# Giving the denominator-spreading matmul 128 rows, 124 of them zero, instead of four, in a linear-attention and MoE kernel

## The chip, the cores and the metric

The kernel runs on one core of a Trainium2 chip. The metric is the device time of one execution in microseconds (us); lower is better.

## The reference

Linear attention over 8 batches of 8 heads (576 tokens, head size 64), followed by a gated feed-forward layer with a three-tap convolution over tokens.

```python
def phi(x):                                   # 64 -> 128, then exp of plus and minus
    proj = np.einsum('bhsd,df->bhsf', x, w_phi)
    proj = proj - np.max(np.abs(proj), axis=-1, keepdims=True)
    return np.concatenate([np.exp(proj), np.exp(-proj)], axis=-1)
q_p, k_p = (phi(q), phi(k))
kv = np.einsum('bhsf,bhsd->bhfd', k_p, v)
z = np.sum(k_p, axis=2)
num = np.einsum('bhsf,bhfd->bhsd', q_p, kv)
den = np.einsum('bhsf,bhf->bhs', q_p, z)[..., None] + 1e-06
x = num / den                                 # heads side by side: [8, 576, 512]
h = np.maximum(x @ w_in, 0.0)                 # 512 -> 1024
conv_out = sum(conv_w[k] * shifted(h, k) for k in range(3))
out = (h * sigmoid(conv_out)) @ w_out         # 1024 -> 512
```

## The kernel before

Names in the profile are those of the program's tiles. Attention works in quads of four heads (two pairs), 16 quads in all, each in five groups of tokens. For each group the tensor engine projects keys and queries (`kp`, `qp`), the vector engine takes the greatest magnitude off, the scalar engine takes exponentials (`ke`, `qe`), queries are transposed (`tp`), keys are multiplied with values (`kv`), and queries with the result (`nm`). Row 64 of `nm` holds the denominators. To keep accuracy, most operands are split into a rounded part and the rest (`..h` and `..l`, type fp32r), and a product takes three matmuls.

For each of the 32 pairs of heads `x_process` then divides. The denominators have been gathered by DMA into `den`; the vector engine takes the reciprocal `rc` and splits it in two parts, and four small DMAs lay these out as four rows of 576 tokens in `rr`: high part of head 0, high part of head 1, low part of head 0, low part of head 1. A matmul with the stationary matrix `sel_r` (four rows of ones and zeros, 128 columns) then adds high and low parts and spreads each head's reciprocal over the 64 partitions that hold the head's numerators. It does so twice per pair, for two chunks of 290 tokens, into the PSUM tile `rb`: 64 such matmuls in the kernel. The vector engine multiplies `num` by `rb` into `xf`, and `xf` is split into `xh` and `xl`, the moving operands of the MoE.

The MoE takes 16 chunks of 288 tokens. `h_part` makes 8 tiles `hp`, each by 12 matmuls of 128 rows, 128 columns and 290 tokens; `conv_process` makes the convolution and the gate on the vector, scalar and GpSimd engines; `o_part` makes 4 tiles `op`, each by 24 matmuls of 288 tokens.

The weights `w_in` and `w_out` arrive as float64. In the first part of the run they are loaded in 16 pieces (`w_r`) and rounded to float32 by the vector, scalar and GpSimd engines (`w_t`), next to the first batch's attention.

The order on each engine is decided ahead: the parts are generators, and a loop merges them, with attention a set number of instructions ahead of the MoE. A scheduler then places each instruction by its own estimates of time, so that a change in one instruction can move others. All loads go out on SyncE's queue (SP), in order. The tile `selr_f`, which receives the four rows of `sel_r` from memory, shares its two buffers (tag `qr`) with the raw queries from the second batch on.

Of the kernel before, what the change touches and what calls it, by code (L numbers as in the profile page):

```python
# [7 lines left out]
F32 = mybir.dt.float32  # L8
# [10 lines left out]
P = 128  # L19
NQ = 2            # quads (four heads each) per batch  # L20
TC = 288          # tokens per MoE chunk
HW = TC + 2       # tokens of h computed per MoE chunk (one token of halo, even width)
VW = D + 1
NH = 11           # tiles of h
# the order of work
WINDOW = 13       # chains of attention in flight
LAT = 1.7         # latencies stretched by
TAIL_US = 24      # of the MoE's products, what is left when attention's are done
AHEAD = 300       # instructions by which attention goes before the MoE that it was merged with
# quads whose products are in float32, as long as the tensor engine has time, so that nothing has to be split  # L30
NQ_F32 = 2        # q's projections
NKV_F32 = 2       # the products with kv


@with_exitstack
def kernel(
    ctx: ExitStack,
    tc: tile.TileContext,
    qT: bass.AP,     # [B, NQ, 128 = (i, d), 2*S], the last 64 tokens of either pair in the middle
    kT: bass.AP,     # likewise  # L40
    vt: bass.AP,     # [B, NQ, 128, 20*65]
    wbd: bass.AP,    # [128, 256] block diagonal of w_phi
    w_in: bass.AP,   # [8 = (4 c, 2 halves), 128, 512], in float64 twice as many words
    conv_w: bass.AP,  # [128, (8, 3)], likewise
    w_out: bass.AP,  # [8, 128, DM], likewise
    ident: bass.AP,  # [128, 128]
    selr: bass.AP,   # [4, 128]
    out: bass.AP,    # [B, 4, 128, S]
):
# [7 lines left out]
    def split(src, hi, lo, eng_hi, eng_lo):  # L57
        """hi: src rounded to 12 significant bits, lo: the exact rest."""
        if eng_hi is nc.scalar:
            nc.scalar.activation(out=hi, in_=src, func=AF.Copy)  # L60
        elif eng_hi is nc.gpsimd:
            nc.gpsimd.tensor_scalar(out=hi, in0=src, scalar1=1.0, scalar2=0.0, op0=ALU.mult, op1=ALU.add)  # L62
        else:
            nc.vector.tensor_copy(out=hi, in_=src)
        eng_lo.tensor_tensor(out=lo, in0=src, in1=hi.bitcast(F32), op=ALU.subtract)  # L65

# [1 line left out]
    def load_const(ap, shape, name):  # L68
# [10 lines left out]
    idn = load_const(ident, [P, P], "idn")  # L79
    selr_f = sb.tile([4, P], F32, name="selr_f", tag="qr", bufs=2)  # L80
    nc.sync.dma_start(out=selr_f, in_=selr)
    sel_r = cp.tile([4, P], F32R, name="sel_r")
    nc.vector.tensor_copy(out=sel_r, in_=selr_f)

    # Weights that come as float64 arrive as raw 64-bit words, of a high half (sign, 11 bits
    # of exponent, 20 of fraction) and a low half (32 of fraction). The engines build
    #   power = +-2^e   and   w = (1.fraction) * power, rounded to float32 once.
    # Exponents below float32's give zero, those above it infinity or NaN.
    bias_e = cp.tile([P, 1], F32, name="bias_e")
# [17 lines left out]
    def weight_split(src, n, hi, lo):  # L107
        """src: [128, 512] weights in DRAM (float32, or the words of float64)."""
        name = f"w{n}_"
        if src.dtype == F32:  # L110
            raw = sb.tile([P, 512], F32, name=f"{name}r", tag="gh", bufs=2)
            nc.sync.dma_start(out=raw, in_=src)
            split(raw, hi, lo, nc.gpsimd, nc.gpsimd)
            return
        raw = sb.tile([P, 1024], I32, name=f"{name}r", tag="gh", bufs=2)
        nc.sync.dma_start(out=raw, in_=src)
        tmp = sb.tile([P, 2, 512], F32, name=f"{name}t", tag="gl", bufs=2)
        w = tmp[:, 0, :]
        float64_round(raw, w, tmp[:, 1, :])
        split(w, hi, lo, nc.scalar, nc.gpsimd)  # L120
# [22 lines left out]

# [1 line left out]
    # The parts below are processes: generators that trace some instructions and then  # L145
    # yield how long the tensor engine is held by them (pe), how long it is until the
    # next part has its operands (wait), or a condition that has to hold (until). The
    # loop at the end merges them into one order in which products of one process
    # cover the latencies of the others.
    now = [0.0]  # L150
# [13 lines left out]

# [1 line left out]
    # A quad is two pairs of heads. Its tokens come in groups: group 0 is the last 64  # L166
    # tokens of both pairs, groups 1 to 4 are 256 tokens of a pair. A tile of 128 tokens
    # holds a pair of heads, one above the other, against block diagonal weights.
    def group_columns(g):
# [15 lines left out]
    def project(n, hi, lo, b, qd, g, kind):  # L185
        """The projection of n tiles of two heads less its greatest magnitude per token and head."""
        if b == 0 and kind == "k":
            # the MoE doesn't use its banks yet
            ps = pm.tile([P, n * 256], F32, name=f"{kind}p{b}_{qd}_{g}", tag="m")
        else:  # L190
            ps = pg.tile([P, n * 256], F32, name=f"{kind}p{b}_{qd}_{g}", tag="g", bufs=4)
# [17 lines left out]
    def after(ins, trace):  # L209
        """Trace an instruction that its engine issues behind ins."""  # L210
        if ins is None:
            return trace()
        with tc.issue_after(ins.ins):
            return trace()
# [5 lines left out]
    def k_process(b, qd, g):  # L220
# [43 lines left out]
        else:  # L264
            # five groups later in the order than the queries with whose products these alternate:
            # the loads of either's weights hide behind the other's products
            kvgen[j] = products()
            set_ready(("ke", j))
            yield until(("kvd", j))
        if g == 4:  # L270
            # these take the place of the same quad's of the batch before
            u = 2 * b + qd
# [27 lines left out]
    def q_process(b, qd, g):  # L300
# [14 lines left out]
        set_ready(("tp", *divmod(j, 5)))  # L315
        # in the order (head, tile) the tokens of a head lie side by side
        tp = pg.tile([P, 2, n, P], F32, name=f"tp{b}_{qd}_{g}", tag="g", bufs=4)
# [14 lines left out]
        yield until(back("num", 1), ("kvq", b, qd), ("ke", j + 5) if paired else None)  # L332
        # pairs of heads in this group, each with its tokens' place in the tile and in the sequence
        parts = [(0, 0, 512, 64), (1, 64, 512, 64)] if g == 0 else [((g - 1) // 2, 0, (g - 1) % 2 * 256, 256)]
# [32 lines left out]
        for pr_, o, s0, w in parts:  # L367
# [3 lines left out]
            dn, nt = den[b, qd, pr_], numt[b, qd, pr_]  # L371
            # denominators in the order (16 tokens, head)
            dro = dr[D : D + 1, 2 * o : 2 * (o + w)]
# [10 lines left out]
    def x_process(b, p):  # L384
# [5 lines left out]
        with tc.high_priority():  # L390
            rc = sb.tile([72, 16], F32, name=f"rc{b}_{p}", tag="rc", bufs=2)
            nc.vector.tensor_scalar(out=dn, in0=dn, scalar1=1e-6, scalar2=None, op0=ALU.add)
            nc.vector.reciprocal(out=rc, in_=dn)
            rr = sb.tile([4, S], F32R, name=f"rr{b}_{p}", tag="rr", bufs=1)
            rhl = [sb.tile([72, 16], F32R, name=f"rc{j}{b}_{p}", tag=f"rc{j}", bufs=2) for j in range(2)]
# [19 lines left out]

# [1 line left out]
    ht = {}  # L417
# [26 lines left out]
    def conv_process(n):  # L444
        c = n % 2
        o = 0 if c == 0 else HW - TC
        for f in range(8):
# [5 lines left out]
            cv = c4[:, f, :]  # L453
            # the tap beyond the batch's first and last token falls on nothing
            nc.gpsimd.tensor_scalar(out=cv, in0=hs[:, o : o + TC], scalar1=cw[:, f, 1:2], scalar2=0.0,  # L455
# [58 lines left out]

# [1 line left out]
    chains = [(0, 0, g, "k") for g in range(5)]  # L516
    for u in range(NQ * B):
        for g in range(5):
            chains.append((*divmod(u, NQ), g, "q"))
            if u + 1 < NQ * B:  # L520
                chains.append((*divmod(u + 1, NQ), g, "k"))
    active = []    # [time, process, is a chain, lead in priority], attention's chains and what they spawn
    lead = [None]
# [12 lines left out]
    def step(p, kind):  # L536
        """Run process p up to its next pause; False when it ended."""
        for what, arg in p[1]:
# [22 lines left out]
    while moe is not None or chains or active:  # L561
        while chains and sum(1 for p in active if p[2]) < WINDOW:
            b, x, g, kind = chains.pop(0)
            # the first batch's attention goes before all else
            lead[0] = AHEAD if b > 0 else None
# [21 lines left out]
        else:  # L587
            # nothing is ready: on to the next time at which something is
            now[0] = min([t for t, _ in ta] + ([tm] if tm is not None else []))
# [56 lines left out]
```

## Time and profile before

| what | value |
|---|---|
| median of 3 runs | 849.68 us (848.51 to 853.46) |
| span of the profiled execution, first to last instruction | 848.8 us |
| what lies around the span | not shown by the profile; the median is 0.9 us above the span |
| tensor engine, matmuls (PE) | 817.7 us busy, 6414 matmuls |
| tensor engine, weight loads (PEld) | 788.2 us |
| vector engine (DVE) | 623.3 us, 1327 instructions |
| scalar engine (ACT) | 571.9 us, 1228 instructions |
| GpSimd (POOL) | 304.0 us, 466 instructions |
| mean granted clock of the tensor engine | 0.981 |

Matmuls overlap each other in the records: one of 290 tokens is shown as lasting some 0.30 us while the next begins 0.13 us after it. What one costs is therefore read from the spacing of starts, not from durations. A weight load has a row of its own (PEld), and a matmul's shape is written as rows*columns of the stationary matrix, then the moving operand.

### The profile page before, as it was taken

How to read it: one execution, taken by the hardware profiler on the slowest of the kernel's cores; microseconds unless marked ns; L12 is line 12 of the kernel's file. 1: busy time of each engine (PE TensorE's matmuls, PEld its weight loads, DVE VectorE, ACT ScalarE, POOL GpSimd, SP SyncE). 2: the span in 40 equal slices, each digit the busy share in tenths (PEclk: the TensorE clock that was granted, in tenths of full speed). 3: DMA queues.
4: the chain of work that ended last, by engine and by line, in shares of the span. 5: the costliest groups of instructions: out<-in, count | busy, mean ns of one | idle time of the engine just before them, and what ended most of it. 6: DMA issues, size and time to landing. Idle time of an engine off the chain costs nothing.

```text
span 848.8 us, 18003 instructions
## 1 busy us (share of the span) xinstructions
PE 817.7 (96%) x6414; PEld 788.2 (93%) x6414; DVE 623.3 (73%) x1327; ACT 571.9 (67%) x1228; POOL 304.0 (36%) x466
## 2 busy tenths in 40 slices
PE   7888879999999999999999999999999999999998
PEld 6867778989999999999999999999999999999998
DVE  5679999898877767776777776777687776756561
ACT  4677787787768667676777867577575876644332
POOL 4557668542442423423142332324144121211110
PEclk9799889999999999999999999999999999999999
DMA  6354331111212212112111211121121100000001
GB/s 194 112 153 125 103 118 51 49 43 53 65 41 65 60 31 68 40 55 56 49 54 47 61 35 57 46 59 54 31 68 36 48 15 22 10 29 29 22 15 49
DMA packets 56336, 49.19 MB, mean 58 GB/s; under 512 B 15028, under 2 KB 54200, under 8 KB 56248
## 3 DMA queue, kind: packets, MB, share of 16 engines
q1 hardware_dynamic: 56248, 48.05, 19.6%
q8 instruction: 51, 0.84, 0.4%
q14 instruction: 37, 0.30, 0.1%
HBM read 38.14 MB, written 9.44 MB: 56 GB/s over the span
## 4 chain that ended last, share of the span: by engine, by line
PE 80%; DVE 9%; ACT 4%; DMA 3%; issue 2%; POOL 0%; SPq 0%; DVEq 0%; POOLq 0%; ACTq 0%
PE op L491 24%; PE hp L432 22%; PE nm L356 8%; PE kv L255 8%; PE tp L320 3%; PE rb L407 2%; PE nm L348 2%; PE qp L199 2%; PE qp L200 2%; PE kp L199 2%; PE qp L201 2%; PE kp L200 2%; PE kp L201 1%; PE kv L251 1%; DMA den<-dr 1%
## 5 line engine op out<-in xcount | busy, mean ns | idle before, releaser
L460 DVE SCALAR_TENSOR_TENSOR c<-h,cw,c 128x288 f32<-128x288 f32 (+1 forms) x256 | 138.6, 550 | 38.4 <-POOL c L455 36.6
L255 PE MATMUL kv<-v,ke 128*128 128x65 f32 x1024 | 161.6, 256 | 0.0
L255 PEld LDWEIGHTS kv<-v,ke 128*128 128x128 f32 x1024 | 156.6, 196 | 4.3 <-issue 1.2
L432 PE MATMUL hp<-xh,win_hi 128*128 128x290 f32 x512 | 153.2, 301 | 1.1 <-ACT os L496 0.6
L432 PE MATMUL hp<-xl,win_hi 128*128 128x290 f32 x512 | 153.5, 300 | 0.0
L455 POOL TENSOR_SCALAR c<-h,cw 128x288 f32<-128x288 f32 x128 | 78.2, 612 | 209.3 <-ACT h L439 172.4
L432 PE MATMUL hp<-xh,win_lo 128*128 128x290 f32 x512 | 153.2, 299 | 0.0
L491 PE MATMUL op<-gh,wout_hi 128*128 128x288 f32 x512 | 152.8, 299 | 0.0
L491 PE MATMUL op<-gh,wout_lo 128*128 128x288 f32 x512 | 151.8, 297 | 0.0
L491 PE MATMUL op<-gl,wout_hi 128*128 128x288 f32 x512 | 151.8, 296 | 0.0
L62 POOL TENSOR_SCALAR kxh<-kr 128x256 fp32r<-128x256 f32 (+1 forms) x80 | 38.0, 475 | 225.7 <-PE kp L200 201.3
L65 DVE TENSOR_TENSOR ql<-qe,qh 128x512 fp32r<-128x512 f32 x112 | 80.1, 728 | 28.2 <-ACT qh L60 28.2
L432 PEld LDWEIGHTS hp<-xh,win_hi 128*128 128x128 f32 x512 | 96.7, 189 | 2.9 <-ACT os L496 1.4
L432 PEld LDWEIGHTS hp<-xh,win_lo 128*128 128x128 f32 x512 | 97.1, 190 | 1.6
L432 PEld LDWEIGHTS hp<-xl,win_hi 128*128 128x128 f32 x512 | 97.0, 189 | 1.0
L491 PEld LDWEIGHTS op<-gh,wout_hi 128*128 128x128 f32 x512 | 96.1, 188 | 0.9
L491 PEld LDWEIGHTS op<-gh,wout_lo 128*128 128x128 f32 x512 | 96.4, 188 | 0.1
L491 PEld LDWEIGHTS op<-gl,wout_hi 128*128 128x128 f32 x512 | 96.2, 188 | 0.2 <-issue 0.2
L439 ACT ACTIVATE h<-hp 128x290 f32<-128x290 f32 x128 | 52.4, 412 | 58.9 <-PE hp L432 56.3
L326 ACT ACTIVATE qe<-tp 128x512 f32<-128x512 f32 x112 | 62.0, 598 | 26.9 <-PE tp L320 22.1
L374 ACT ACTIVATE dr<-nm 1x512 f32<-1x512 f32 (+1 forms) x96 | 46.3, 482 | 48.2 <-PE nm L356 28.2
L204 DVE TENSOR_REDUCE km<-kp 128x4 f32<-128x512 f32 (+1 forms) x80 | 50.4, 631 | 33.8 <-PE kp L201 33.8
(86 smaller groups left out, 2039.1 us busy)
## 6 DMA issues: line engine op xcount, KB each, us to landing
v<-in_vt_dram SPq DMA_DIRECT2D x80, 130.0 KB
out_dram<-os SPq DMA_DIRECT2D x64, 144.0 KB
kr<-in_kT_dram SPq DMA_DIRECT2D x64, 128.0 KB
qr<-in_qT_dram SPq DMA_DIRECT2D x64, 128.0 KB
w_r<-in_w_in_dram SPq DMA_DIRECT2D x8, 512.0 KB
w_r<-in_w_out_dram SPq DMA_DIRECT2D x8, 512.0 KB
rr<-rc SPq DMA_DIRECT2D x128, 2.2 KB
kr<-in_kT_dram SPq DMA_DIRECT2D x16, 64.0 KB
```

The source lines that it names most:

```text
L62: nc.gpsimd.tensor_scalar(out=hi, in0=src, scalar1=1.0, scalar2=0.0, op0=ALU.mult, op1=ALU.add)
L65: eng_lo.tensor_tensor(out=lo, in0=src, in1=hi.bitcast(F32), op=ALU.subtract)
L204: nc.vector.tensor_reduce(out=m, in_=ps3, axis=AX, op=ALU.max, apply_absolute_value=True)
L255: ins = nc.tensor.matmul(out=kp[i][:, s, p0 : p0 + VW], lhsT=lhsT, rhs=v[:, (2 * t + i) * VW : (2 * t + i + 1) * VW], start=False, stop=(g ...
L326: nc.scalar.activation(out=e, in_=tp.rearrange("p i t s -> p i (t s)"), func=AF.Exp, scale=1.0 - 2.0 * s)
L356: ins = after(ins, lambda: nc.tensor.matmul(out=ps[:, i, o : o + w], lhsT=w_, rhs=x_, start=(k == 0), stop=(k == 5)))
L374: nc.scalar.activation(out=dro.rearrange("o (r i c) -> o i r c", i=2, c=16), in_=ps[D : D + 1, :, o : o + w].rearrange("o i (r c) -> o i r ...
L432: nc.tensor.matmul(out=ps, lhsT=w_, rhs=x_, start=(k == 0), stop=(k == 11))
L439: nc.scalar.activation(out=hs, in_=ps, func=AF.Relu)
L455: nc.gpsimd.tensor_scalar(out=cv, in0=hs[:, o : o + TC], scalar1=cw[:, f, 1:2], scalar2=0.0, op0=ALU.mult, op1=ALU.add)
L460: nc.vector.scalar_tensor_tensor(out=cv[:, lo:hi], in0=hs[:, o + j - 1 + lo : o + j - 1 + hi], scalar=cw[:, f, j : j + 1], in1=cv[:, lo:hi ...
L491: nc.tensor.matmul(out=ps, lhsT=w_, rhs=x_, start=(k == 0), stop=(k == 23))
```

## The change

`sel_r` and `rr` get all 128 partitions. Rows 4 to 127 are set to zero once, at the start; the four rows that matter are written as before. `rr` is now a single tile for the whole run, where it was allocated anew for each pair from a pool of one buffer. The conversion of `sel_r` moves from the vector engine to GpSimd, which also does the two memsets. The matmul's code is the same; its operands have 128 rows.

```diff
-    selr_f = sb.tile([4, P], F32, name="selr_f", tag="qr", bufs=2)
-    nc.sync.dma_start(out=selr_f, in_=selr)
-    sel_r = cp.tile([4, P], F32R, name="sel_r")
-    nc.vector.tensor_copy(out=sel_r, in_=selr_f)
+    selr_f = sb.tile([P, P], F32, name="selr_f", tag="qr", bufs=2)
+    nc.gpsimd.memset(selr_f, 0.0)
+    nc.sync.dma_start(out=selr_f[:4, :], in_=selr)
+    sel_r = cp.tile([P, P], F32R, name="sel_r")
+    nc.gpsimd.tensor_copy(out=sel_r, in_=selr_f)
+    rr = cp.tile([P, S], F32R, name="rr")
+    nc.gpsimd.memset(rr.bitcast(F32), 0.0)
...
-            rr = sb.tile([4, S], F32R, name=f"rr{b}_{p}", tag="rr", bufs=1)
```

The rest of the diff takes comments out. Line numbers grow by three or four: the matmul is line 407 before and 410 after.

The order of the engines changes in the first third of the program and is nearly the same from there on. At the start of SyncE's queue stood, before (`kr` and `qr` are raw keys and queries, named by batch, quad and group):

```order
L75 DMA wbd_f_70<-in_wbd_dram 128x256
L179 DMA kr0_0_0_131<-in_kT_dram 128x128
L176 DMA qr0_0_0_147<-in_qT_dram 128x128
L179 DMA kr0_0_1_139<-in_kT_dram 128x256
L176 DMA qr0_0_1_149<-in_qT_dram 128x256
L230 DMA v0_0_0_137<-in_vt_dram 128x260
L179 DMA kr0_0_2_188<-in_kT_dram 128x256
```

And now:

```order
L75 DMA wbd_f_70<-in_wbd_dram 128x256
L183 DMA qr1_0_0_853<-in_qT_dram 128x128
L180 DMA qr0_0_0_150<-in_qT_dram 128x128
L183 DMA kr0_0_0_134<-in_kT_dram 128x128
L180 DMA qr0_0_1_152<-in_qT_dram 128x256
L183 DMA kr0_0_1_142<-in_kT_dram 128x256
L234 DMA v0_0_0_140<-in_vt_dram 128x260
```

The first keys have moved from second to fourth place, behind a load of the second batch's queries. On GpSimd, a little later, among the splits of the first keys, the conversion of `sel_r` now stands:

```order
L62 TENSOR_SCALAR kxh0_0_4_306<-kr0_0_4_304 128x256
L85 CAST sel_r_81<-selr_f_78 128x128
L65 TENSOR_TENSOR kxl0_0_4_307<-kr0_0_4_304,kxh0_0_4_306 128x256
```

It delays the split behind it by its own time. On the vector engine the conversion of the weights has moved ahead of attention's work. Before, from the engine's 23rd row on (`w0_t`, `w1_t` are weights; `km`, `qs`, `ks` attention's):

```order
L206 TENSOR_TENSOR qs0_0_2_322<-qp0_0_2_317,qm0_0_2_320 128x512
L103 SCALAR_TENSOR_TENSOR cw_84<-cw_84,cw_raw_85 128x24
L96 TENSOR_SCALAR w1_t_153<-w1_r_151 128x512
L204 TENSOR_REDUCE km0_0_4_380<-kp0_0_4_373 128x4
L206 TENSOR_TENSOR qs0_0_3_329<-qp0_0_3_324,qm0_0_3_327 128x512
L204 TENSOR_REDUCE km0_1_0_391<-kp0_1_0_387 128x2
L98 TENSOR_SCALAR w0_t_121<-w0_r_119 128x512
```

And now:

```order
L210 TENSOR_TENSOR qs0_0_2_325<-qp0_0_2_320,qm0_0_2_323 128x512
L102 TENSOR_SCALAR w0_t_124<-w0_r_122 128x512
L104 SCALAR_TENSOR_TENSOR w0_t_124<-w0_r_122,w0_t_124 128x512
L100 TENSOR_SCALAR w1_t_156<-w1_r_154 128x512
L210 TENSOR_TENSOR qs0_0_3_332<-qp0_0_3_327,qm0_0_3_330 128x512
L107 SCALAR_TENSOR_TENSOR w0_t_124<-w0_t_124,w0_r_122 128x512
L208 TENSOR_REDUCE km0_0_4_383<-kp0_0_4_376 128x4
```

The lead grows: the last weight's last instruction is the vector engine's 213th before and its 177th now, 36 places earlier. From about the 1,900th of 5,662 tensor engine instructions on, the order there is the same but for single places at `rb`.

## The prediction

> **What bounds the kernel.** I read the page's busy times first, then the busy time in two stretches, split where the vector engine stops being full.
>
> ```profile
> PE 817.7 (96%) x6414; PEld 788.2 (93%) x6414; DVE 623.3 (73%) x1327; ACT 571.9 (67%) x1228; POOL 304.0 (36%) x466
> ```
>
> ```profile
> 0.00:143.50 143.50, 121.74 (x836) 110.30 (x837) 119.16 (x217) 103.35 (x222) 91.14 (x112) 0.89 0.42 125
> 143.50:849.00 705.50, 695.99 (x5580) 677.92 (x5579) 504.16 (x1111) 468.50 (x1006) 212.90 (x355) 1.00 0.16 44
> ```
>
> The columns are PE, PEld, DVE, ACT and POOL busy with their counts, then granted clock and DMA. From 143.5 us on PE is busy for 696.0 of 705.5 us at full clock, and the next engine, DVE, for 504.2 (71%). There the tensor engine is the bound, and what it saves in spacing the run saves. Before 143.5 us no engine is full all the time: the stretch is paced by loads, weight conversion and chains between engines.
>
> The affected matmul, by the view of its tile, and its count in the two stretches:
>
> ```profile
> L407 PEld LDWEIGHTS rb<-rr,sel_r x64: 181/181/185, 68.1 to 745.3; 4*128 4x128 f32 x64
> L407 PE MATMUL rb<-rr,sel_r x64: 288/396/400, 68.1 to 745.4; 4*128 4x290 f32 x64
> ```
>
> ```profile
> 143.50:849.00 705.50, 21.10 (x56) 9.88 (x56) 1.00 0.16 44
> ```
>
> So 56 of the 64 stand in the stretch that PE bounds. Their load of 181 ns is nothing special. What they cost shows only in the spacing around one. The timeline of PE, and of its weight loads, in the middle of a run of `hp` (columns: start, busy, engine, line):
>
> ```profile
> 248.03 0.29 PE L432 MATMUL hp<-xh,win_hi 128*128 128x290 f32 x1
> 248.16 0.29 PE L432 MATMUL hp<-xl,win_hi 128*128 128x290 f32 x1
> 248.38 0.40 PE L407 MATMUL rb<-rr,sel_r 4*128 4x290 f32 x1
> 248.71 0.40 PE L432 MATMUL hp<-xh,win_lo 128*128 128x290 f32 x1
> 248.94 0.30 PE L432 MATMUL hp<-xh,win_hi 128*128 128x290 f32 x1
> 249.08 0.30 PE L432 MATMUL hp<-xl,win_hi 128*128 128x290 f32 x1
> ```
>
> ```profile
> 248.03 0.19 PEld L432 LDWEIGHTS hp<-xl,win_hi 128*128 128x128 f32 x1
> 248.38 0.18 PEld L407 LDWEIGHTS rb<-rr,sel_r 4*128 4x128 f32 x1 [0.16 <-ACT ke L237]
> 248.71 0.19 PEld L432 LDWEIGHTS hp<-xh,win_lo 128*128 128x128 f32 x1
> 248.81 0.19 PEld L432 LDWEIGHTS hp<-xh,win_hi 128*128 128x128 f32 x1
> ```
>
> Ordinary `hp` start 0.13 us apart, because each one's load runs a step ahead of its matmul: the load for the matmul at 248.16 began at 248.03. `rb`'s load begins only at 248.38, with its own matmul, and the next `hp`'s load only at 248.71, again with its own matmul. The reader is to see that the lead of the loads is lost twice, going into the four-row matmul and coming out, and must be built up again. From 248.16 to 248.94 three steps take 0.78 us where three ordinary ones take 0.40: an excess of 0.38 us.
>
> **The change part by part.**
>
> *The 64 matmuls.* Moving shape and columns stay (290, 128); the rows become 128. The changed one is then of the very shape of `hp`, 128*128 with 128x290 of the same type, and the trace shows that at 0.13 us. I take an excess of zero. The lower bound is the same, since nothing here is cheaper than `hp` for that shape. The upper bound is today's excess, if the loss is not due to the rows.
>
> The excess depends on the neighbours, so I weigh three kinds. The 56 are 46 single ones and five pairs of two in a row, counted along the timeline from the first at 143.9 to the last at 745.4 us. Of the single ones, 38 stand as above, with the full 0.38, and 8 have a short neighbour after `nm` or `kv`, as here:
>
> ```profile
> 184.38 0.31 PE L356 MATMUL nm<-qh,kvl 128*65 128x256 f32 x1
> 184.62 0.40 PE L407 MATMUL rb<-rr,sel_r 4*128 4x290 f32 x1
> 184.94 0.33 PE L356 MATMUL nm<-qh,kvh 128*65 128x256 f32 x1
> 185.12 0.33 PE L255 MATMUL kv<-v,ke 128*128 128x65 f32 x2
> ```
>
> ```profile
> 375.25 0.31 PE L356 MATMUL nm<-qh,kvl 128*65 128x256 f32 x1
> 375.40 0.30 PE L432 MATMUL hp<-xh,win_hi 128*128 128x290 f32 x1
> ```
>
> 184.38 to 185.12 is 0.74 us. The same without loss: 0.15 from `nm` to an `hp` (second fence), 0.13 for the `hp` shape, 0.12 from `nm` to `kv`, the shortest such step: 0.40. Excess 0.34. A pair, and the one pair with a wait inside:
>
> ```profile
> 641.94 0.30 PE L432 MATMUL hp<-xh,win_lo 128*128 128x290 f32 x1
> 642.16 0.54 PE L407 MATMUL rb<-rr,sel_r 4*128 4x290 f32 x2
> 642.63 0.33 PE L356 MATMUL nm<-qh,kvh 128*65 128x256 f32 x1
> 642.80 0.28 PE L199 MATMUL kp<-wbd_hi,kxh 128*128 128x256 f32 x1
> ...
> 543.12 0.37 PE L407 MATMUL rb<-rr,sel_r 4*128 4x290 f32 x1 [0.47 <-DVE ks L206]
> ```
>
> 641.94 to 642.80 is 0.86 us for four steps, against 3 x 0.13 + 0.15 = 0.55: excess 0.31 for the pair. The 0.47 us in the pair at 543 is a wait for DVE and stays. Sum: 38 x 0.38 + 8 x 0.34 + 5 x 0.31 = 14.4 + 2.7 + 1.6 = 18.7 us off the stretch from 143.5 us.
>
> The Trainium skill's page "TensorEngine Tiling (Array Packing)", Key Properties, says that a change of tiling mode drains the tensor engine, which would make an excess of this kind at each side of a four-row matmul; the two late loads agree with it. Its page "TensorE: Matmul & The Clock Gate", Part 2, step 1, speaks against this change: a weight load takes as long with few rows as with 128, and its summary table has one short-row matmul at the time of a full one. The loads here, 181 ns against 0.19 us, agree with that, the spacing does not; by that rule alone neither the 18.7 nor the gain on the early ones would come, and the sum would be 851.0.
>
> *The eight early ones.* They lie at 68 to 123 us, where DVE paces; between 0 and 8 x 0.38 = 3.0 us can come from them. I take 1.0, nearer the covered end, as DVE decides there.
>
> *The first loads.* The start of the chain of waits and SP's first issues:
>
> ```profile
> 1.18 2.61 DMA kr<-in_kT_dram
> ```
>
> ```profile
> 1.18 0.42 SPq L179 DMA_DIRECT2D kr<-in_kT_dram  x1
> 1.65 0.43 SPq L176 DMA_DIRECT2D qr<-in_qT_dram  x1
> 2.12 0.43 SPq L179 DMA_DIRECT2D kr<-in_kT_dram  x1
> ```
>
> The first keys now go out two places later, at 2.12: +0.94 us on the chain.
>
> *The new GpSimd work.* Nearest rows, the old conversion of four rows and a first split of 128x128:
>
> ```profile
> L83 DVE CAST sel_r<-selr_f x1: 514/514/514, 11.8 to 11.8; 4x128 fp32r<-4x128 f32 x1
> ...
> 3.88 0.30 POOL L62 TENSOR_SCALAR kxh<-kr 128x128 fp32r<-128x128 f32 x1 [3.05 <-DMA kr<-in_kT_dram]
> ```
>
> The conversion sits in front of a split on the chain: 0.30 to 0.51 us; I take +0.4. The memset of 128x576 (4.5 times the columns of the 0.30 us row: at most 1.4 us) hides in GpSimd's 3.05 us of idle time before the first keys; without that cover it would cost the 1.4. SP's load of `selr_f` waits for the small memset, which is long over when SP reaches it.
>
> *The single `rr` tile.* The old pool had one buffer, so its four DMAs already waited for both matmuls of the pair before. Nothing is added; if it were, `rb` would wait for the landing instead.
>
> *The moved order.* Up to the point where the orders agree again each engine does the same work. Weights come earlier on DVE, attention later. I take 0, and bounds: a gain up to the 5.3 us that DVE stood before a weight in the first 60 us, a loss up to 36 displaced places at DVE's mean of 119.16 / 217 = 0.55 us, 19.8 us.
>
> ```profile
> DVE w_t L96 <- POOL win_lo L65: 5.3, 2, 3.6
> ```
>
> *Sum.* 848.8 - 18.7 - 1.0 + 0.94 + 0.4 = 830.4 us of span. The median of the runs stands 0.9 us above the profiled span; with that, 831.3 us.
>
> **The rivals.**
>
> *The loss is not due to the rows.* The load row of `rb` carries a wait of 0.16 us, and each `rb` stands behind several semaphores. If the lateness came from these, a matmul of four rows would cost what one of 128 does, and only the startup's terms would be left: 848.8 + 0.94 + 0.4 + 0.9 = 851.0. Against it: the second late load, the `hp` at 248.71, follows a matmul for which it has nothing to wait, and the step into `rb` is 0.22 to 0.24 us in all three timelines above, whatever stands before. If only the entry step (0.09 of 0.38) is a wait, 56 x 0.09 = 5.0 us stay: 836.3. The rule of the Trainium skill's page "TensorE: Matmul & The Clock Gate" on few rows stands on the side of this rival.
>
> *The startup gives it back* (the other side). The weights' lead pushes the first batches' attention back on DVE, PE starves, and the full stretch begins later. At the bound of 19.8 us the time is 831.3 + 19.8 = 851.1, slower than before. It decides from 18.4 us on. For it speaks that DVE is in order and that the tensor engine's clock was already only 0.89 there; against it, that DVE idled 143.5 - 119.2 = 24.3 us in this stretch, time which earlier weights can fill.
>
> *PE's saved time turns into waits.* If another engine held back half of it, 831.3 + 9.4 = 840.7. DVE at 71% and ACT at 66% from 143.5 us on speak against it.
>
> **How the numbers follow.** Forecast, with startup between -5 and +5 us: 0.75. Entry step stays a wait or saved time half lost: 0.11. Startup loses 5 to 14 us: 0.06. Nothing gained by the rows: 0.04. Startup at its bound: 0.02. Startup gains more than 5 us: 0.02. Likeliest 831.3; the range goes down by 5.3 and some more to 825, and up to the half-lost case, 841. A measurement of this kernel tells about 0.5%, 4.2 us, from no change. Faster takes the first, most of the second and third and the last: 0.93; same 0.05; slower 0.02.
>
> **What would show it.** `rb` should stand as 128*128 at 0.13 us spacing, its load ahead of its matmul, the next `hp` too; durations near 300 instead of 396 ns. The stretch from the first full PE to the end should be some 19 us shorter, with the same order. Its beginning should lie within 5 us of 143.5. The prediction is wrong if `rb`'s load still starts with its matmul, if PE's idle time after 143.5 us grows, or if the full stretch begins late.

## The result and the profile after

The changed kernel takes 837.6 us (median of 5), against 849.7 us before: a ratio of 0.985 (95% interval 0.982 to 0.987), some 12.5 us faster. The prediction said 831.3 us, with a range of 825 to 841.

One of the five executions, the one that was profiled, ran at a mean granted clock of 0.75 and took 957.1 us, so the ratio is that of the other four, and the profile shown here is a second one of the same kernel at the usual clock: 835.2 us of span in an execution of 837.0 us. Its busy times, from the page, and its two stretches, cut where about as many matmuls are left as at the cut before (5583 and 5580):

```profile
PE 801.9 (96%) x6414; PEld 784.3 (94%) x6414; DVE 623.7 (75%) x1326; ACT 573.1 (69%) x1228; POOL 307.5 (37%) x469
```

```profile
0.00:145.80 145.80, 121.63 (x833) 109.07 (x834) 120.63 (x221) 106.32 (x225) 95.64 (x117) 0.91 0.41 123
145.80:835.20 689.40, 680.25 (x5583) 675.19 (x5581) 503.06 (x1106) 466.82 (x1004) 211.90 (x353) 1.00 0.16 45
```

The affected matmul, by its tile:

```profile
L410 PEld LDWEIGHTS rb<-rr,sel_r x64: 186/188/288, 69.8 to 731.9; 128*128 128x128 f32 x64
L410 PE MATMUL rb<-rr,sel_r x64: 291/298/610, 69.8 to 732.0; 128*128 128x290 f32 x64
```

Three things are to be seen. The matmul's median fell from 396 to 298 ns, that of an `hp`. PE's busy time fell by 15.8 us (817.7 to 801.9), the span by only 13.6. And the stretch in which PE is full got 15.9 us shorter (705.3 to 689.4 us, to the last instruction) but began 2.3 us later.

### The profile page after: what moved, and what is told of

It reads as the page before. It is cut to its first block, busy times and chain, and to the rows that moved or that the text cites. A ratio compares the mean times of both kernels' runs of the same rounds, so it can differ in the third digit from the quotient of the medians.

```text
span 955.3 us, 18005 instructions
## 1 busy us (share of the span) xinstructions
PE 937.9 (98%) x6414; PEld 920.7 (96%) x6414; DVE 622.2 (65%) x1326; ACT 576.6 (60%) x1228; POOL 294.1 (31%) x469
## 4 chain that ended last, share of the span: by engine, by line
PE 93%; DVE 3%; ACT 2%; issue 1%; DMA 1%; POOL 0%; SPq 0%; ACTq 0%
PE op L494 26%; PE hp L435 25%; PE kv L259 10%; PE nm L360 9%; PE tp L324 4%; PE nm L352 3%; PE kp L203 2%; PE kp L204 2%; PE kp L205 2%; PE qp L204 2%; PE qp L203 2%; PE qp L205 2%; PE kv L255 2%; PE rb L410 1%; PE qp L200 1%
## 5 line engine op out<-in xcount | busy, mean ns | idle before, releaser
L259 PEld LDWEIGHTS kv<-v,ke 128*128 128x128 f32 x1024 | 181.8, 221 | 5.2
L259 PE MATMUL kv<-v,ke 128*128 128x65 f32 x1024 | 181.8, 280 | 0.0
L463 DVE SCALAR_TENSOR_TENSOR c<-h,cw,c 128x287 f32<-128x287 f32 (+1 forms) x256 | 138.6, 550 | 59.1 <-POOL c L458 57.3
L435 PE MATMUL hp<-xl,win_hi 128*128 128x290 f32 x512 | 171.0, 334 | 0.0
L435 PE MATMUL hp<-xh,win_hi 128*128 128x290 f32 x512 | 170.9, 335 | 0.1
L494 PE MATMUL op<-gh,wout_hi 128*128 128x288 f32 x512 | 170.5, 333 | 0.0
L494 PE MATMUL op<-gh,wout_lo 128*128 128x288 f32 x512 | 170.3, 333 | 0.0
L494 PE MATMUL op<-gl,wout_hi 128*128 128x288 f32 x512 | 170.3, 333 | 0.0
L435 PE MATMUL hp<-xh,win_lo 128*128 128x290 f32 x512 | 170.1, 332 | 0.0
L435 PEld LDWEIGHTS hp<-xh,win_hi 128*128 128x128 f32 x512 | 104.4, 205 | 1.0 <-ACT os L499 0.6
```

The costliest lines, as they stand in the source:

```text
L259: ins = nc.tensor.matmul(out=kp[i][:, s, p0 : p0 + VW], lhsT=lhsT, rhs=v[:, (2 * t + i) * VW : (2 * t + i + 1) * VW], start=False, stop=(g ...
L435: nc.tensor.matmul(out=ps, lhsT=w_, rhs=x_, start=(k == 0), stop=(k == 11))
L463: nc.vector.scalar_tensor_tensor(out=cv[:, lo:hi], in0=hs[:, o + j - 1 + lo : o + j - 1 + hi], scalar=cw[:, f, j : j + 1], in1=cv[:, lo:hi ...
L494: nc.tensor.matmul(out=ps, lhsT=w_, rhs=x_, start=(k == 0), stop=(k == 23))
```

## The experiments

Two theories stood at the start. A: the rows are worth the predicted 18 to 19 us, and the new order of the first third gives 5 to 7 back. B: the order is neutral, and the rows are worth only 12 to 13.

**The changed kernel again.**

> The changed kernel once more, for a profile at full clock. Both theories: 837 us, 12 to 13 below the kernel before, rb at 0.13 us spacing with its load ahead of it. Theory A (the rows are worth 18 to 19 us from 143.5 us on, as predicted, and the new order of the first third gives 5 to 7 back): the stretch that the tensor engine fills begins 5 to 7 us later than before. Theory B (the order is neutral and the rows are worth only 12 to 13): it begins at 143 to 145 us, and idle time of the tensor engine behind it grows.

It took 837.1 us, a ratio of 0.9851 (0.9835 to 0.9867) to the kernel before. The late beginning is there, but it is 2.3 us, not the 5 to 7 that A needs.

**128 rows in the old order.** With `sel_r` converted as before, the scheduler's order is that of the kernel before on every engine, but for two memsets on GpSimd.

```diff
 selr_f = sb.tile([4, P], F32, name="selr_f", tag="qr", bufs=2)
 nc.sync.dma_start(out=selr_f, in_=selr)
-sel_r = cp.tile([4, P], F32R, name="sel_r")
-nc.vector.tensor_copy(out=sel_r, in_=selr_f)
+sel_r = cp.tile([P, P], F32R, name="sel_r")
+nc.gpsimd.memset(sel_r.bitcast(F32), 0.0)
+nc.vector.tensor_copy(out=sel_r[:4, :], in_=selr_f)
+rr = cp.tile([P, S], F32R, name="rr")
+nc.gpsimd.memset(rr.bitcast(F32), 0.0)
...
-            rr = sb.tile([4, S], F32R, name=f"rr{b}_{p}", tag="rr", bufs=1)
```

> 128 rows as in the changed kernel, but the four rows of sel_r are loaded and converted as before, on the vector engine, so that every engine keeps the order of the kernel before (GpSimd has two memsets more). Theory A: 849.7 - 18.7 - 0 to 1 = 830 to 831 us, some 6 us faster than the changed kernel. Theory B: 837 us, as the changed kernel.

It took 835.1 us, ratio 0.9823 (0.9805 to 0.9841): between the two theories. The rows alone are worth 15.0 us (850.1 to 835.1, medians of the same chip).

**Four rows in the new order.** The counterpart: the changed kernel, with a matmul of four rows.

```diff
-nc.tensor.matmul(out=rb, lhsT=sel_r, rhs=rr[:, t0 : t0 + HW], start=True, stop=True)
+nc.tensor.matmul(out=rb, lhsT=sel_r[:4, :], rhs=rr[:4, t0 : t0 + HW], start=True, stop=True)
```

> The changed kernel with its order and memsets, but the matmul reads only the first four rows of sel_r and rr. Theory A: 849.7 + 5 to 7 = 855 to 857 us, slower than the kernel before. Theory B: 850 us, as the kernel before.

It took 852.2 us, ratio 1.0025 (1.0013 to 1.0037): the order alone costs 2.1 us. The four kernels make a square, and it closes:

| median, us | old order | new order | order costs |
|---|---|---|---|
| four rows | 850.1 | 852.2 | 2.1 |
| 128 rows | 835.1 | 837.1 | 2.0 |
| the rows gain | 15.0 | 15.1 | |

Both theories had a part wrong. The order costs less than A said but is not free, and the rows give more than B said but less than the 19.7 us predicted (18.7 from the full stretch and 1.0 before it).

**Where the missing gain went.** The old-order pair has the same matmuls in the same order, so the two timelines can be laid on each other one matmul at a time. Around a single `rb` in 128 rows, PE and its loads:

```profile
244.91 0.29 PE L434 MATMUL hp<-xl,win_hi 128*128 128x290 f32 x1
245.04 0.30 PE L409 MATMUL rb<-rr,sel_r 128*128 128x290 f32 x1
245.18 0.30 PE L434 MATMUL hp<-xh,win_lo 128*128 128x290 f32 x1
245.31 0.30 PE L434 MATMUL hp<-xh,win_hi 128*128 128x290 f32 x1
```

```profile
244.91 0.19 PEld L409 LDWEIGHTS rb<-rr,sel_r 128*128 128x128 f32 x1
245.04 0.19 PEld L434 LDWEIGHTS hp<-xh,win_lo 128*128 128x128 f32 x1
```

These are the matmuls that stood at 248.16 to 248.94 before. The steps are now 0.13, 0.14 and 0.13 us, and each load starts a step ahead of its matmul. The whole 0.38 us is gone here, as at most of the single places.

The sum over the full stretch is read from a matmul just ahead of its first `rb` to one just behind its last. Before:

```profile
143.55 0.33 PE L255 MATMUL kv<-v,ke 128*128 128x65 f32 x2
...
745.90 0.29 PE L491 MATMUL op<-gh,wout_lo 128*128 128x288 f32 x1
```

With 128 rows in the old order, the same two:

```profile
142.15 0.33 PE L258 MATMUL kv<-v,ke 128*128 128x65 f32 x2
...
729.94 0.29 PE L493 MATMUL op<-gh,wout_lo 128*128 128x288 f32 x1
```

602.35 us became 587.79: 14.6 us for the 56, where 18.7 were predicted. The missing 4.1 us sit at few places. The largest, in the kernel before and then with 128 rows:

```profile
162.04 0.40 PE L407 MATMUL rb<-rr,sel_r 4*128 4x290 f32 x1
...
163.01 0.29 PE L432 MATMUL hp<-xh,win_lo 128*128 128x290 f32 x1
163.23 0.40 PE L407 MATMUL rb<-rr,sel_r 4*128 4x290 f32 x1
```

```profile
160.82 0.29 PE L434 MATMUL hp<-xh,win_lo 128*128 128x290 f32 x1
162.20 0.38 PE L409 MATMUL rb<-rr,sel_r 128*128 128x290 f32 x1 [1.08 <-DVE ks L209]
```

The second `rb` now arrives 1.08 us before the vector engine has released it. The subtraction that releases it, before and then with 128 rows:

```profile
161.79 0.68 DVE L206 TENSOR_TENSOR ks<-kp,km 128x512 f32<-128x512 f32 x1
```

```profile
161.38 0.68 DVE L209 TENSOR_TENSOR ks<-kp,km 128x512 f32<-128x512 f32 x1
```

It came only 0.41 us earlier, while the tensor engine came to the second `rb` more than 2 us earlier: the `hp` ahead of it starts at 160.82 and not at 163.01 us. Of this, 1.40 us had been won before the full stretch (it begins at 142.15 and not at 143.55). So around 162 us the vector engine decides, and what the tensor engine saves there is not saved by the run. Here the two `rb` with their neighbours lose 0.69 us instead of winning 0.7. At four of the five pairs the saving is partly a wait as well. The pair that took 0.86 us for four steps at 641.94:

```profile
629.26 0.30 PE L434 MATMUL hp<-xh,win_lo 128*128 128x290 f32 x1
629.40 0.43 PE L409 MATMUL rb<-rr,sel_r 128*128 128x290 f32 x2
629.67 0.28 PE L359 MATMUL nm<-qh,kvh 128*65 128x256 f32 x1
629.94 0.36 PE L202 MATMUL kp<-wbd_hi,kxh 128*128 128x256 f32 x1
```

Up to `nm` all is as predicted (0.41 us from the `hp`). Then `kp` starts 0.27 us after `nm`, where 0.12 us would be a plain step: its sequencer stands for 0.40 us in a wait for a semaphore, from 629.49 to 629.88. The same wait was there before, from 642.16 to 642.55, and had ended by the time at which `nm` began at 642.63. The shortfalls, from the matmul-by-matmul comparison:

| place | predicted us | found us | short by |
|---|---|---|---|
| the two `rb` at 162 and 163 us | -0.72 | +0.69 | 1.4 |
| `rb` at 250.1, the next `nm` waits | -0.38 | +0.04 | 0.4 |
| three `rb` behind a `kp`, which still wait | -1.14 | -0.42 | 0.7 |
| five pairs | -1.55 | -0.96 | 0.6 |
| five `rb` between `kv` and `nm` | -1.70 | -1.39 | 0.3 |
| matmuls that are no neighbours of `rb` | 0 | +0.8 | 0.8 |

They add up to 4.2 us; the other 35 `rb` gave what was predicted, 13.3 us. In the first two rows and at four of the pairs a wait took the saving. Behind `kp` the load engine still stands idle for 0.21 us ahead of `rb`'s load with 128 rows, as it did before; the profile puts this down to the scalar engine's `qe`. Between `kv` and `nm` the price was off by a little. The last row is made of small shifts and was not followed up.

**64, 32 and 65 rows.** What is it about four rows? Three kernels with the changed kernel's order, differing from it only in the rows that the matmul reads, as in the diff above.

> The changed kernel, its matmul reading the first 64 rows. If any part of the array less than the whole loses the lead of the loads: rb's load starts with its matmul, the excess is 0.38 us as with four rows, and the time is that of new_order_4 (855 under theory A, 850 under B). If only a quarter of the rows does: the time of the changed kernel, 837 us.

> The changed kernel, its matmul reading the first 32 rows. Both: steps of 0.22 and 0.33 us as with 4 and 64 rows, 851 to 854 us. If instead a full group of rows kept the lead: 837 us.

> The changed kernel, its matmul reading the first 65 rows. If the lead of the loads is lost whenever fewer than 128 rows are used: rb at 0.22 and 0.33 us steps, 852 to 854 us as with 64 rows. If it hangs on whether the rows need the whole array (more than half): steps of 0.13 us and the changed kernel's 837 us.

The first two took 853.7 and 851.8 us, beside 852.2 with four rows; 65 rows took 833.8 us (one run each; 32 and 65 rows ran on another chip, on which the kernel before took 849.5 us instead of 850.1). The steps tell it apart from the scatter. PE and its loads with 64 rows:

```profile
277.45 0.29 PE L494 MATMUL op<-gh,wout_lo 128*128 128x288 f32 x1
277.67 0.40 PE L410 MATMUL rb<-rr,sel_r 64*128 64x290 f32 x1
278.00 0.40 PE L494 MATMUL op<-gh,wout_hi 128*128 128x288 f32 x1
278.24 0.30 PE L494 MATMUL op<-gl,wout_hi 128*128 128x288 f32 x1
```

```profile
277.67 0.18 PEld L410 LDWEIGHTS rb<-rr,sel_r 64*128 64x128 f32 x1 [0.17 <-issue]
278.00 0.19 PEld L494 LDWEIGHTS op<-gh,wout_hi 128*128 128x128 f32 x1
```

The same place with 65 rows:

```profile
270.11 0.29 PE L494 MATMUL op<-gh,wout_lo 128*128 128x288 f32 x1
270.24 0.29 PE L410 MATMUL rb<-rr,sel_r 65*128 65x290 f32 x1
270.37 0.30 PE L494 MATMUL op<-gh,wout_hi 128*128 128x288 f32 x1
270.51 0.29 PE L494 MATMUL op<-gl,wout_hi 128*128 128x288 f32 x1
```

```profile
270.11 0.19 PEld L410 LDWEIGHTS rb<-rr,sel_r 65*128 65x128 f32 x1
270.24 0.19 PEld L494 LDWEIGHTS op<-gh,wout_hi 128*128 128x128 f32 x1
```

64 rows cost 0.79 us for three steps, 65 rows 0.40. With 32 rows the steps are those of 64, 0.22, 0.33 and 0.24 us. The border lies between 64 and 65 rows: with 65 the matmul stands in the stream like any other. The Trainium skill's page "TensorEngine Tiling (Array Packing)" lists arrays of 32 and 64 rows as modes beside the whole, and its Key Properties say that a change of mode drains the engine; loads that wait for the matmul ahead of them, on both sides, at 4, 32 and 64 rows and not at 65 or 128, agree with it. No record names a mode, so that this is what happens inside the engine is argued and not shown. What the pairs add is that the price hangs on the change from one kind of matmul to the other: in the pair at 642 us the first four-row load starts late, with its matmul, but the second starts at 642.27, 0.13 us ahead of its matmul at 642.40, as after any late load, and the load of `nm` behind them is late again. And the pair at 745 us, between `op`, gave back 0.38 us for its two matmuls, as a single place does.

**Which part of the order costs the 2 us.** The profiles of the square can be compared by the number of matmuls done. Up to the 839th all four have run as many into each tile. It starts at 143.69 and 147.45 us with four rows, in the old and the new order, and at 142.29 and 146.26 with 128: the new order is 3.8 and 4.0 us behind. At the 2,462nd, an `rb` in all four, it is 1.9 and 2.4 us behind, and 2.1 and 2.4 at the last. So the startup loses some 4 us, and about half of them come back soon after. Time at half clock does not explain it alone: in the first 160 us it is 30.7 and 27.3 us with four rows, 23.9 and 27.3 with 128.

To find the part of the order, two kernels of 128 rows were run. One is the old-order version, with the keys loaded first, but converts `sel_r` on GpSimd:

```diff
 nc.gpsimd.memset(sel_r.bitcast(F32), 0.0)
-nc.vector.tensor_copy(out=sel_r[:4, :], in_=selr_f)
+nc.gpsimd.tensor_copy(out=sel_r[:4, :], in_=selr_f)
```

> 128 rows; the first loads go out as before (keys first), but sel_r is converted on GpSimd, which moves instructions of every engine over the whole run. If the order's 2 us come from the first loads (keys 0.94 us later), 835 us, as with the old order. If from the conversion on GpSimd, 836 to 837. If any reshuffle of the startup moves the time by some us either way, it can be anywhere between 830 and 840.

and one that is the changed kernel, but converts on the vector engine:

```diff
-nc.gpsimd.tensor_copy(out=sel_r, in_=selr_f)
+nc.vector.tensor_copy(out=sel_r, in_=selr_f)
```

> 128 rows; the first loads as in the changed kernel (the second batch's queries first), but sel_r is converted on the vector engine. If the order's 2 us come from the first loads, 837 us, as the changed kernel. If from the conversion on GpSimd, 835 us. If any reshuffle moves the time, anywhere between 830 and 840.

They took 835.1 us, ratio 0.9839 (0.9816 to 0.9863), and 839.0 us, ratio 0.9872 (0.9854 to 0.9890). The two with the keys first are at 0.982 and 0.984, the two with the other queries first at 0.985 and 0.987. This points to the first loads and away from the conversion on GpSimd. It isn't settled: the intervals overlap, these two ran on another chip than the square, and each edit also moved other instructions.

One thing that goes with the scatter of these times is seen in two kernels with the same order of matmuls throughout, the changed one and the one with 65 rows (one profile each, on two chips), in their first 145 us (granted clock is the third number from the end):

```profile
0.00:145.00 145.00, 120.83 (x825) 108.27 (x826) 119.83 (x220) 105.67 (x224) 94.92 (x116) 0.91 0.41 123
```

```profile
0.00:145.00 145.00, 119.39 (x853) 107.17 (x854) 124.74 (x223) 107.57 (x228) 95.69 (x117) 0.94 0.42 125
```

The 3.2 us between their spans (835.2 and 832.0) all lie ahead of 136 us; from there on the two run in step to within 0.1 us. In the first 160 us the granted clock was at half for 27.3 us in the one and 17.1 us in the other. The changed kernel falls behind most at two places, by 2.3 us from 29 to 34 us and by 1.2 us from 127 to 131 us, and at both its clock is at half (until 34.2, and from 126.4 to 129.8 us) where the other's is full. In both profiles each drop to half clock in the startup follows 3.4 us in which the matmul records leave 0.8 to 1.9 us idle. Gaps as long are also followed by full clock (1.6 us in either), so when the clock drops is not told by the gaps alone.

## Why the prediction was right, and where it missed

- *The bound.* Right but for a few places. From 143.5 us on PE set the time nearly everywhere, and nearly all of the gain came from there; around 162 us the vector engine did.
- *The cause.* Right: the loss lies in the late loads at both sides of the short-row matmul, not in semaphore waits of `rb`. With 128 rows the same `rb`, with the same waits, keeps a load a step ahead of it. The rival that the rows do not matter fell with 15.0 us.
- *The price of a single place.* Right: 0.38 us, or 0.34 beside a short neighbour, gone as predicted at 35 of the 46 single places.
- *The sum over the stretch.* This is the term that was mis-sized: 18.7 us predicted, 14.6 found. The step that failed is "I take an excess of zero" for all places alike. At 162, 250 and at four of the pairs a wait that had lain hidden came into view, and three `rb` behind a `kp` kept a wait that had been counted as loss. That is the third rival, in small: it was priced at half the saving, and these rows fell short by 3.1 of the 18.7 us, a sixth. The waits of the stretch could have been looked up beforehand: the 0.40 us that `kp` stands behind the pair at 642 was in the trace of before.
- *The eight early ones.* 1.0 us predicted. The medians leave 15.0 - 14.6 = 0.4, and the two profiles show 1.4 (143.55 to 142.15), with 30.7 and 23.9 us at half clock in that part. Whether 1.0 was right can't be told from this.
- *The startup.* +1.34 us predicted for the first loads and the conversion, 2.0 and 2.1 found. The first key load went out at 2.12 us, as predicted, and the first split began at 4.69 instead of 3.88 us. But the tensor engine did not stand still for it: it began at 3.98 us with the queries, where it had begun at 4.23 with the keys. And the conversion ran at 12.29 us, behind five of the splits of the first keys. So the paths that the two terms were taken from are not shown, and with 4 us lost by the 839th matmul and half of them won back, that the sum lies near 2 us is in part luck. The 0 taken for the moved order stays open with it; its bound of 19.8 us was far off.
- *The time around the span.* The profiled execution took 1.8 us more than its span, in the changed kernel, and not the 0.9 that came of setting one execution's span beside the median of others. This left an error of under 1 us in the sum.

Put together: 849.7 - 15.0 + 2.0 = 836.7, beside 837.1 and 837.6 measured; the terms are read off the runs, so this is a sum that closes and no second prediction. The likeliest change, 18.4 us, was half as large again as the real one. The old-order version, at 835.1 us, is the better form of the change, faster than both kernels.

## What to carry to other kernels

In a stream of full-array matmuls, look at the spacing on both sides of a matmul with 64 rows or fewer, not at its duration: here a single one cost 0.38 us more than its 0.13, two in a row no more than that together, and zero rows up to 65 or 128 took that away for two memsets at the start. Before counting such a saving in full, look for the waits that end during the stall or shortly after it; they come into view when it goes. And when a constant's setup is edited under a scheduler, compare the whole order: keeping the four-row load and its conversion as they were kept every engine's order and 2 us.

## What the runs showed of the hardware that was not expected

That the border lies between 64 and 65 rows, with no step from 4 to 32 to 64. That two four-row matmuls in a row pay no more than one (0.38 us in the pair at 745 us): the second's load has its lead of 0.13 us again, though the step to it is still 0.24 us, as behind other late loads, and the lead is lost anew behind the pair. And that the startups of two kernels with the same order of matmuls differed by 3.2 us, with 10 us more at half clock in the slower one.
